# Four edits to a gated-attention and mixer kernel: four first loads, two weight tiles at another place in the queue, four blocks mixed together, and two branch hints

## The chip, the cores and the metric

The kernel runs on 1 core of one Trainium2 chip. The metric is the device time of one execution, in microseconds (us). Three executions of the kernel before took 471.62, 471.79 and 471.83 us; the median is 471.79 us.

## The reference

A linear attention with a forget gate (4 batches, 8 heads, 768 steps, head size 48) is followed by a mixer with a low-rank mix over time and a two-layer channel network (width 384, inner width 1536). In short:

```
f = sigmoid(f_logit)
for t: state = f[t] * state + outer(k[t], v[t]);  y[t] = q[t] @ state
x = y, heads side by side              # (4, 768, 384)
h = (x^T @ U @ V)^T                    # U 768x32, V 32x768: mixes the 768 steps
u = x + h
out = u + relu(u @ w_ch1) @ w_ch2      # w_ch1 384x1536, w_ch2 1536x384
```

q, k, v and f_logit are float32. The weights of the mixer are float64 in HBM.

## The kernel before

The 32 (batch, head) pairs are handled two at a time, as 16 units of two heads, four units for each batch. A unit is loaded as f, k, q and v, the gates are turned into logs and summed over time with a triangular matrix on PE (line 790), keys and queries are turned by PE (line 744) and scaled by DVE (line 758), and then come scores (926), kept keys (953), states (974), the scan over chunks on DVE (996), and the two products that give y (1012 and 1030). ACT moves results out of PSUM and takes the logs and exponentials. The first four units, batch 0, run alone; from then on the attention of batch b+1 is filled in between the matrix products of the mixer of batch b. PE, ACT and DVE follow an order written out by hand for the first batches, and PE for the whole program; later DVE and ACT are ordered by a scheduler, in which the additions of the mixer are given priority (`add`).

**The start.** Line 640 clears `blank`, 384 columns of zeros. PE multiplies it with itself three times (`busy(3)`, line 1133) to have something to do while the first f is loaded. `load(0, "f", "k", "q")` (line 641) issues two DMAs for f, one for each head, then one for k and one for q, all on the queue of SP. Unit 0 treats its f in two halves of three blocks each: DVE clamps them (line 775), ACT takes Exp and Ln (777 and 779), and PE sums them (790).

**The weights.** `weight_loader` (line 82 to 101) brings a float64 tile in and ACT, DVE and POOL turn it into float32. U is `weights[0]`, V is `weights[1:3]`, and the 12 tiles of w1 follow. The first six of these go into room that is not yet in use, tiles of the pool `zp` called `zw`: two of them are asked for at once and issued after V of unit 3's loads (end of the branch `n == 1`), the other four in `held()`, where a copy by ACT of one element of `x` (line 1150) makes SP wait until that point of ACT's program. SP issues its DMAs in order, and waits at most for the one it has to wait for; what stands behind it waits too.

**The mix.** After the low-rank product h (two matmul groups, `low_rank` and `added_up`), `mix(t)` multiplies block t of V with h. There are six blocks of 128 steps; V is stored as four row groups of 32 rows, so blocks 0 to 3 lie in different row groups of PE, and blocks 4 and 5 lie in groups 0 and 1 again. `mix(t)` works in pairs: two blocks go into one PSUM tile of two banks (pool `ps_big`, three such tiles), and DVE adds both to x in one instruction of 768 columns (line 204). For batch 3 the three pairs (`self.mixes`) are laid one by one between the products of the piece before (`fewer`, line 468, a scheme with 15 products in place of 18, whose results DVE combines); the four sums of the next piece (`ready`, 768 columns each) are queued on DVE ahead of all of them.

**The end.** `ok` tells whether the factored path was safe. Each engine reads it into a register (line 1603) and jumps over the general path, which is a second whole program, at line 1604. Then all engines meet and end. POOL, ACT and PE reach their jump long before DVE and SP.

Of the kernel before, what the change touches and what calls it, by code (L numbers as in the profile page):

```python
# [10 lines left out]
F32 = mybir.dt.float32  # L11
# [4 lines left out]
ALU = mybir.AluOpType  # L16
# [140 lines left out]
class Mixer:  # L157
# [6 lines left out]
    def __init__(self, tc, b, x, U, V, w1, w2, sums, ident, blocks, out, two, three, zp, ps_big, ps_mm, wide=False,  # L164
                 z_all=None, room=None, pair=0):
        nc = tc.nc
        P = nc.NUM_PARTITIONS
        NCH, DM = x.shape[1], x.shape[2]
        R, FF = U.shape[2], w1.shape[2]
        NG = P // R  # L170
# [4 lines left out]
        uT, z, h, S = {}, {}, {}, {}  # L175
# [30 lines left out]
        pu = {}  # L206

        def mix(t):

            s = t % 2  # L210
            if s == 0:
                pu[0] = ps_big.tile([P, 2, 512], F32, name="pu", tag="big")
            g = slice((t % NG) * R, (t % NG + 1) * R)
            nc.tensor.matmul(pu[0][:, s, 0:DM], lhsT=V[g, t // NG, :], rhs=h[1][g, :], start=True, stop=True)  # L214
            if s == 1:
                add(x[:, t - 1 : t + 1, :], x[:, t - 1 : t + 1, :], pu[0][:, :, 0:DM], ALU.add)


        hs, last = {}, {}

# [273 lines left out]
            return [(4 * NDC * 2 * P, lambda j=j: ch1(a, j)) for j in range(NI)]  # L494


        parts = [low_rank, added_up, lambda: [mix(t) for t in range(NCH)]]
        parts += [lambda a=a: turn(a) for a in range(NA)]
        self.before = [(DM, piece) for piece in parts]

# [4 lines left out]
        for a in range(NA - 1):  # L505
            ahead = first(a + 1)
            self.main += ready(a) + ahead[: NI // 2] + halved(a) + ahead[NI // 2 :]
        self.main += ready(NA - 1)
        self.after = second(NA - 1)
        self.mixes = [(DM, lambda t=t: [mix(t), mix(t + 1)]) for t in range(0, NCH, 2)]  # L510
        self.first, self.second, self.ready, self.fewer, self.halved = first, second, ready, fewer, halved
        self.sums_of_x = lambda a: [(1, lambda: sums_of_x(a))]

# [24 lines left out]
def factored_path(ctx, tc, q, k, v, f_logit, moe_U, moe_V, moe_w_ch1, moe_w_ch2, out, ok):  # L538
# [4 lines left out]
    nc = tc.nc  # L543
    B, H, S, D = q.shape
    P = nc.NUM_PARTITIONS
    C = P // 2
    NCH = S // C

    NBL = S // P
    HP = H // 2  # L550
    DM = H * D
    R = moe_U.shape[1]
# [21 lines left out]
    ps_big = ctx.enter_context(tc.tile_pool(name="ps_big", bufs=3, space=bass.MemoryType.PSUM))  # L574
    ps_mm = ctx.enter_context(tc.tile_pool(name="ps_mm", bufs=2, space=bass.MemoryType.PSUM))
# [60 lines left out]
                        in_=head[:, :, part * NB : part * NB + n_ch],  # L636
                    )

    blank = late[:, 5, 0 : 3 * P]
    nc.vector.memset(blank, 0.0)  # L640
    load(0, "f", "k", "q")
    load(1, "f")
    load(0, "v")

# [50 lines left out]
    early = len(weights)  # L695
# [10 lines left out]
    FIRST = 6  # L706
# [419 lines left out]
    with tc.manual_schedule(engines={nc.vector.engine, nc.scalar.engine}):  # L1126
# [3 lines left out]

        def busy(n, cols=DM):
            for _ in range(n):
                nc.tensor.matmul(idle[:, 0:cols], lhsT=blank[:, 0:P], rhs=blank[:, 0:cols], start=True, stop=True)

        written = ExitStack()
        written.enter_context(tc.manual_schedule(engines={nc.sync.engine}))
# [7 lines left out]
        halves, join = [[w[i] for w in weights[:early]] for i in (2, 3)]  # L1144
        done, rest = slice(0, 2 * (HP - 1) * D), slice(2 * (HP - 1) * D, DM)

        def held():
            for i in range(2, FIRST, 2):
                t = zp.tile([P, NFC // 2, 2 * P], F32, name="zw").rearrange("p i t -> p (i t)")
                nc.scalar.copy(t[:, 0:1], x_tiles[0][:, 0, 0:1])  # L1150
                spare.extend([t.bitcast(U64)[:, 0:WP], t.bitcast(U64)[:, WP : 2 * WP]])
            for load_w in weights[early + 2 : early + FIRST]:
                load_w[0]()
            load(HP, "f", "k", "q", "v")

        for n in range(HP):
            last = n + 1 == HP
            pieces = rear(n - 1, "scan") + front(n, "unpack_q", "keys") + rear(n, "spread") + rear(n - 1, "read")
            if last:
                pieces += join[:1] + halves[1:2]  # L1160
            elif n:
                pieces += front(n + 1, "gates")
            pieces += front(n, "queries") + rear(n, "kept")
            if n == 0:
                pieces += [lambda: busy(1, P)] + front(1, "gates", "gates_end") + rear(0, "scores", "mask")
                pieces += front(1, "unpack_k") + rear(0, "states")
            elif last:
                pieces += join[1:2] + halves[2:] + rear(n - 1, "inner") + rear(n, "states")
                pieces += join[2:] + rear(n, "scan") + [held] + rear(n, "scores", "mask")
            else:  # L1170
                pieces += front(n + 1, "gates_end", "unpack_k", "unpack_q") + rear(n - 1, "inner") + rear(n, "states")
            if n + 2 == HP:
                pieces += halves[:1]
            if not last:
                pieces += front(n + 1, "read_back")
                pieces += rear(n, "scan", "scores", "mask") if n else []
                pieces += front(n + 1, "keep")
            for piece in pieces:
                piece()
            if n == 0:  # L1180
                load(2, "k", "q")
                load(3, "f")
                load(2, "v")
            elif n == 1:
                weights[0][0]()
                load(3, "k", "q")
                for load_w in weights[1:early]:
                    load_w[0]()
                load(3, "v")
                for load_w in weights[early : early + 2]:  # L1190
                    load_w[0]()
        m = mixer(0)
        low_rank_of, added_up_of, mix_of, turn_of, ch1_of = m.some
        for load_w in weights[early + FIRST : early + FIRST + 4]:
# [75 lines left out]
    def of(i, kind):  # L1270
        if i >= len(pairs):
            return []
        b, a = pairs[i]
        return getattr(mixers[b], kind)(a)
# [5 lines left out]
    for i in range(len(pairs)):  # L1280
        ahead, behind = of(i + 1, "fewer"), of(i, "second")
        nxt = of(i + 2, "sums_of_x")
        if not ahead:
            todo += behind
            break
        todo += of(i, "ready")
        if i == 0:
            todo += [p for two_of in zip(ahead, low[:2] + mixers[1].mixes) for p in two_of] + behind[:1] + low[3:4] + nxt
        else:
            todo += (low[4:] if i == 1 else []) + ahead[:4] + nxt + ahead[4:5]  # L1290
            if i + 2 < len(pairs):
                todo += behind[:1]
        if i + 2 < len(pairs):
            todo += ahead[5:6] + behind[1:2] + ahead[6:7] + behind[2:3] + ahead[7:] + behind[3:]
        else:
            todo += ahead[5:6] + behind[:1] + ahead[6:] + behind[1:2] + of(i + 1, "ready") + behind[2:]
# [284 lines left out]
@with_exitstack  # L1581
def kernel(
    ctx: ExitStack,
    tc: tile.TileContext,
    q: bass.AP,
    k: bass.AP,
    v: bass.AP,
    f_logit: bass.AP,
    moe_U: bass.AP,
    moe_V: bass.AP,  # L1590
    moe_w_ch1: bass.AP,
    moe_w_ch2: bass.AP,
    out: bass.AP,
):


    nc = tc.nc
    args = (q, k, v, f_logit, moe_U, moe_V, moe_w_ch1, moe_w_ch2, out)
    flag = ctx.enter_context(tc.tile_pool(name="flag", bufs=1))
    ok = flag.tile([1, 1], I32, name="ok")  # L1600
    with ExitStack() as inner:
        factored_path(inner, tc, *args, ok)
    good = nc.values_load(ok[0:1, 0:1], min_val=0, max_val=1)
    with tc.If(good == 0):
        with ExitStack() as inner:
            general_path(inner, tc, *args)

# [29 lines left out]
```

## Time and profile before

One profiled execution took 471.81 us. Its span, from the first to the last instruction, is 470.0 us, so 1.8 us lie around it; the times below are in that span.

| | us | share |
|---|---|---|
| span | 470.0 | |
| PE busy | 456.2 | 97% |
| DVE busy | 352.3 | 75% |
| ACT busy | 165.6 | 35% |
| POOL busy | 54.2 | 12% |
| PE idle, 0 to 10 us | 3.3 | |
| PE idle, 10 to 44 us | 2.2 | |
| PE idle, 44 to 160 us | 0.8 | |
| PE idle, 160 to 320 us | 1.1 | |
| PE idle, 320 to 360 us | 1.0 | |
| PE idle, 360 us to the end | 5.4 | |

A line of a timeline has the start and the duration of a group in us, its engine, its line in the kernel, the operation, what it writes and reads, the number of instructions, and in brackets the idle time of its engine just before it with what ended that idle time. Names that end in q (SPq, DVEq) are the sequencers, which issue DMAs, wait and branch. One float32 matmul of the program shows as two instructions.

### The profile page before, as it was taken

The numbers are of one execution on the slowest core, as the hardware profiler recorded it, in microseconds if no ns is written. First come the engines' busy times: TensorE is split into PE (matmuls) and PEld (weight loads), VectorE is DVE, ScalarE is ACT, GpSimd is POOL, SyncE is SP. The second block draws the span as 40 slices with busy tenths as digits, with TensorE's granted clock in tenths as the row PEclk, the third lists the DMA queues.
The fourth block names the chain that finished last, engine by engine and source line by source line (L and its number), as shares of the span: only waits on it lengthen the run. The fifth ranks groups of instructions, "written<-read, shape, count | busy, mean of one in ns | idle before, by whom it ended". The sixth has DMA issues, their size and how long they took to land.

```text
span 470.0 us, 13005 instructions
## 1 busy us (share of the span) xinstructions
PE 456.2 (97%) x5639; PEld 394.9 (84%) x5639; DVE 352.3 (75%) x579; ACT 165.6 (35%) x315; POOL 54.2 (12%) x60
## 2 busy tenths in 40 slices
PE   7999999999999999999999999999999999999995
PEld 5876888875666578999898878989979999999995
DVE  5767788979999677775675659977796877759632
ACT  5775776562332144322323133232312312112200
POOL 2002445634112001010101001020000000000000
PEclk9999999999999999999999999999999999999999
DMA  9947997577678504506334020000000000000001
GB/s 194 209 107 191 226 220 179 155 116 106 120 120 130 83 18 52 77 7 110 48 66 73 7 52 19 12 3 20 18 1 1 35 1 35 0 16 20 1 36 40
DMA packets 148313, 34.36 MB, mean 73 GB/s; under 512 B 136790, under 2 KB 146710, under 8 KB 148246
## 3 DMA queue, kind: packets, MB, share of 16 engines
q1 hardware_dynamic: 148246, 33.44, 36.4%
q8 instruction: 46, 0.75, 0.7%
q14 instruction: 21, 0.17, 0.1%
HBM read 28.70 MB, written 4.72 MB: 71 GB/s over the span
## 4 chain that ended last, share of the span: by engine, by line
PE 75%; DVE 13%; issue 3%; ACT 3%; DMA 2%; SPq 2%; POOL 0%; DVEq 0%; ACTq 0%; POOLq 0%
PE pw L365 25%; PE pz L279 18%; PE pp L468 12%; PE po L331 5%; PE y L1012 2%; PE y L1030 2%; PE ds L974 1%; PE sc L926 1%; PE pt L744 1%; PE pt L790 1%; SPq L634 1%; PE pu L214 1%; DVE late L845 1%; DMA v_nat<-in_v_dram 1%; DVE kz L721 1%
## 5 line engine op out<-in xcount | busy, mean ns | idle before, releaser
L279 PE MATMUL pz<-uT,w 128*128 128x256 f32 x492 | 111.5, 382 | 0.3
L279 PEld LDWEIGHTS pz<-uT,w 128*128 128x128 f32 x492 | 91.7, 190 | 12.9 <-ACT uT L268 0.6
L1000 POOL COPY st<-added 128x576 f32<-128x576 f32 x12 | 18.2, 1513 | 188.0 <-DVE added L996 188.0
L365 PE MATMUL pw<-zw,w_raw 128*128 128x192 f32 x216 | 38.0, 329 | 0.0
L365 PE MATMUL pw<-w,z_all 128*128 128x192 f32 x216 | 37.3, 327 | 0.0
L101 POOL TENSOR_TENSOR w<-w_y,w_r 128x384 int32<-128x384 int32 x24 | 31.5, 1313 | 39.5 <-DVE w_y L100 23.2
L365 PEld LDWEIGHTS pw<-w,z_all 128*128 128x128 f32 x216 | 35.3, 190 | 0.5
L365 PEld LDWEIGHTS pw<-zw,w_raw 128*128 128x128 f32 x216 | 35.1, 190 | 0.6 <-issue 0.3
L314 ACT ACTIVATE z_all<-pz 128x512 f32<-128x512 f32 x33 | 19.6, 598 | 45.1 <-PE pz L279 44.6
L827 DVE TENSOR_TENSOR_SCAN late<-fz,late 128x768 f32<-128x768 f32 x12 | 21.1, 1756 | 7.3 <-ACT fz L822 7.1
L461 ACT ACTIVATE other<-other 128x512 f32<-128x512 f32 x18 | 11.3, 631 | 40.3 <-DVE other L204 40.3
L331 PE MATMUL po<-w,zw 128*128 128x384 f32 x72 | 25.2, 495 | 0.0
L331 PE MATMUL po<-w,z_all 128*128 128x384 f32 x72 | 24.7, 493 | 0.0
L939 DVE TENSOR_TENSOR A<-sc,causal 128x768 f32<-128x768 f32 x16 | 15.2, 952 | 9.5 <-PE sc L926 9.5
L845 DVE TENSOR_TENSOR_SCAN late<-fz,other 128x768 f32<-128x768 f32 x12 | 22.0, 1834 | 0.2
L331 PEld LDWEIGHTS po<-w,zw 128*128 128x128 f32 x72 | 13.2, 190 | 9.6 <-issue 0.8
L331 PEld LDWEIGHTS po<-w,z_all 128*128 128x128 f32 x72 | 13.3, 190 | 8.9 <-DVE o L204 0.6
L981 ACT COPY added<-ds 48x576 f32<-48x576 f32 (+1 forms) x28 | 17.8, 635 | 5.1 <-PE ds L974 4.7
L461 ACT ACTIVATE z_all<-z_all 128x512 f32<-128x512 f32 x12 | 7.6, 630 | 33.3 <-DVE z_all L204 33.3
L468 PE MATMUL pp<-v_nat,late 128*128 128x128 f32 x152 | 19.1, 275 | 0.0
L1012 PEld LDWEIGHTS y<-st,qT 48*64 48x64 f32 x704 | 13.6, 137 | 6.4 <-issue 3.9
L98 DVE TENSOR_SCALAR w_y<-w_y 128x384 f32<-128x384 f32 (+3 forms) x27 | 12.1, 448 | 8.9 <-ACT w_y L91 8.9
(224 smaller groups left out, 867.3 us busy)
## 6 DMA issues: line engine op xcount, KB each, us to landing
w_raw<-in_moe_w_ch_dram SPq DMA_DIRECT2D x18, 384.0 KB, 4.1
out_dram<-o SPq DMA_DIRECT2D x24, 192.0 KB, 2.0
v_nat<-in_v_dram SPq DMA_DIRECT2D x16, 144.0 KB, 4.3
v_nat<-in_v_dram SPq DMA_DIRECT2D x32, 72.0 KB, 3.9
zw<-in_moe_w_ch_dram SPq DMA_DIRECT2D x6, 384.0 KB, 5.1
w<-in_k_dram SPq DMA_DIRECT2D x4, 288.0 KB, 3.7
w<-in_q_dram SPq DMA_DIRECT2D x4, 288.0 KB, 5.1
late<-in_f_logit_dram SPq DMA_DIRECT2D x10, 96.0 KB, 3.0
```

Source lines behind the costliest of these rows:

```text
L101: nc.gpsimd.tensor_tensor(dst.bitcast(I32), shaped(y.bitcast(I32)), shaped(r), ALU.add)
L279: nc.tensor.matmul(pm[:, i * 2 * P : (i + 1) * 2 * P], lhsT=w1[:, m, o : o + P], rhs=uT[a][:, m, :], start=(m == 0), stop=(m == NDC - 1))
L314: nc.scalar.activation(z[a, c][:, k : k + 2, :].rearrange("p i t -> p (i t)"), pm, AF.Relu)
L331: nc.tensor.matmul(pm, lhsT=z[a, i // NI][:, i % NI, s * P : (s + 1) * P], rhs=w2[:, i, :], start=(i == 0), stop=(i == NFC - 1))
L365: nc.tensor.matmul(W["pm"][:, n * HM : (n + 1) * HM], lhsT=lhs[:, i, :], rhs=rhs[:, i, :], start=(i == 0), stop=(i == NI - 1))
L461: nc.scalar.activation(dst, dst, AF.Relu, scale=float(SIGNS[n]))
L468: nc.tensor.matmul(pm[:, i, r * P : (r + 1) * P], lhsT=room["w"](wn)[:, r * P : (r + 1) * P], rhs=x_node(a, xn), start=((xn, wn) == of[0]) ...
L827: nc.vector.tensor_tensor_scan(backwards(X, S - 1, S), backwards(f, S, S), backwards(ends, S - 1, S), 0.0, ALU.mult, ALU.add,)
L845: nc.vector.tensor_tensor_scan(Y, f[:, 0:S], starts, 0.0, ALU.mult, ALU.add)
L981: nc.scalar.copy(added[r, 1:].rearrange("p (e c s) -> p e c s", c=NBL, s=2), ds[r, :, 0 : NBL * D].rearrange("p s (c e) -> p e c s", e=D),)
L1000: nc.gpsimd.tensor_copy(st, states.rearrange(by_e, c=NCH))
L1012: nc.tensor.matmul(o(c % 2, par, c // 2), lhsT=T["q"][rows[par], chunk[c]], rhs=T["st"][rows[par], c, :], start=(c <= 2), stop=False, skip ...
```

## The change

1. **Four first loads.** f of unit 0 comes in four DMAs in place of two: for each half (three blocks) one DMA for each head, the one head on the queue of SP, the other on that of ACT. `blank` is one column, which the busy matmuls read again and again (`broadcast_to`).
2. **V and the first two w1 tiles.** Their loads move from the end of the round n == 1 to the head of the round n == 3. In SP's program V now stands behind v of unit 3, and the two w1 tiles wait for a new one-element copy by ACT, which stands behind the copy of line 808 of unit 3.
3. **Four blocks at once.** For batches 2 and 3, `mix_four` puts blocks 0 and 1 into one tile of `ps_big` and blocks 2 and 3 into one tile each of `ps_mm`; DVE adds 768, 384 and 384 columns. Blocks 4 and 5 go as before. For batch 3 there are two pieces between the products in place of three, and `ready` moves behind one more product piece; in DVE's program the last of its four sums moves from ahead of the products' combinations to behind the additions of blocks 2 and 3.
4. **Hints.** A hint that the jump of line 1604 will be taken, on DVE and SP. It has no dependences: in the built program it is the first instruction of both engines.

```diff
+        def mix_product(dst, t):
+            g = slice((t % NG) * R, (t % NG + 1) * R)
+            nc.tensor.matmul(dst, lhsT=V[g, t // NG, :], rhs=h[1][g, :], start=True, stop=True)
+
+        def mix_four():
+            big = ps_big.tile([P, 2, 512], F32, name="pu", tag="big")
+            pms = [big[:, s, :] for s in range(2)] + [ps_mm.tile([P, 512], F32, name="pu1", tag="mm") for _ in range(2)]
+            for t, pm in enumerate(pms):
+                mix_product(pm[:, 0:DM], t)
+            add(x[:, 0:2, :], x[:, 0:2, :], big[:, :, 0:DM], ALU.add)
+            for t in range(2, NG):
+                add(x[:, t, :], x[:, t, :], pms[t][:, 0:DM], ALU.add)
+
+        def mix_blocks():
+            first = 0
+            if b > 1 and sums is not None:
+                mix_four()
+                first = NG
+            for t in range(first, NCH):
+                mix(t)
...
-        parts = [low_rank, added_up, lambda: [mix(t) for t in range(NCH)]]
+        parts = [low_rank, added_up, mix_blocks]
...
-        self.mixes = [(DM, lambda t=t: [mix(t), mix(t + 1)]) for t in range(0, NCH, 2)]
+        self.mixes = [(DM, mix_four), (DM, lambda: [mix(t) for t in range(NG, NCH)])]
...
-    blank = late[:, 5, 0 : 3 * P]
+    blank = late[:, 5, 0:1]
     nc.vector.memset(blank, 0.0)
-    load(0, "f", "k", "q")
+    queues = nc.sync, nc.scalar
+    for m in range(2):
+        some = slice(m * NBL // 2, (m + 1) * NBL // 2)
+        for par in range(2):
+            queues[par].dma_start(out=nat[0]["f"][:, some, par, 0:D],
+                                  in_=f_logit[0, par].rearrange("(c p) d -> p c d", p=P)[:, some, :])
+    load(0, "k", "q")
...
-                nc.tensor.matmul(idle[:, 0:cols], lhsT=blank[:, 0:P], rhs=blank[:, 0:cols], start=True, stop=True)
+                nc.tensor.matmul(idle[:, 0:cols], lhsT=blank.broadcast_to((P, P)), rhs=blank.broadcast_to((P, cols)),
+                                 start=True, stop=True)
...
-        def held():
-            for i in range(2, FIRST, 2):
+        def room_for(first, last):
+            for i in range(first, last, 2):
                 t = zp.tile([P, NFC // 2, 2 * P], F32, name="zw").rearrange("p i t -> p (i t)")
                 nc.scalar.copy(t[:, 0:1], x_tiles[0][:, 0, 0:1])
                 spare.extend([t.bitcast(U64)[:, 0:WP], t.bitcast(U64)[:, WP : 2 * WP]])
-            for load_w in weights[early + 2 : early + FIRST]:
+            for load_w in weights[early + first : early + last]:
                 load_w[0]()
+
+        def held():
+            room_for(2, FIRST)
             load(HP, "f", "k", "q", "v")
...
             if last:
-                pieces += join[:1] + halves[1:2]
+                pieces = [w[0] for w in weights[1:early]] + [lambda: room_for(0, 2)] + pieces + join[:1] + halves[1:2]
...
                 load(3, "k", "q")
-                for load_w in weights[1:early]:
-                    load_w[0]()
                 load(3, "v")
-                for load_w in weights[early : early + 2]:
-                    load_w[0]()
...
-        todo += of(i, "ready")
         if i == 0:
-            todo += [p for two_of in zip(ahead, low[:2] + mixers[1].mixes) for p in two_of] + behind[:1] + low[3:4] + nxt
+            todo += [p for two_of in zip(ahead, low[:2] + mixers[1].mixes) for p in two_of] + ahead[4:5]
+            todo += of(0, "ready") + behind[:1] + low[3:4] + nxt
         else:
-            todo += (low[4:] if i == 1 else []) + ahead[:4] + nxt + ahead[4:5]
+            todo += of(i, "ready") + (low[4:] if i == 1 else []) + ahead[:4] + nxt + ahead[4:5]
...
+    tc.mark_branch_hint_location("general", "LikelyTaken", engines=[nc.vector.engine, nc.sync.engine])
     good = nc.values_load(ok[0:1, 0:1], min_val=0, max_val=1)
-    with tc.If(good == 0):
+    with tc.If(good == 0, label="general"):
```

## The prediction

> **What bounds the kernel now.** I read the page first, then PE's waits, then the chain of waits, and the timeline wherever a wait of PE lies in the stretch of an edit.
>
> ```profile
> PE 456.2 (97%) x5639; PEld 394.9 (84%) x5639; DVE 352.3 (75%) x579; ACT 165.6 (35%) x315; POOL 54.2 (12%) x60
> PE   7999999999999999999999999999999999999995
> ```
>
> PE is full except in the first and the last slice: 13.8 us of the span are idle, at the front, at the end and in a few gaps. No edit removes PE work, so each can win only a gap. The granted clock is full in every slice. PE's waits name the gaps:
>
> ```profile
> PE pt L790 <- ACT late L779: 1.2, 1, 1.2
> PE sc L926 <- issue: 1.0, 1, 1.0
> ...
> PE pu L214 <- DVE x L204: 0.6, 1, 0.6
> PE pp L468 <- DVE qT L204: 0.4, 1, 0.4
> ```
>
> The columns are the total, the count and the longest. The first is the start, the second a wait that nothing in the profile explains, the last two the mix of batch 3. The chain of waits shows the start (start and duration in us):
>
> ```profile
> 1.32 3.39 DMA late<-in_f_logit_dram
> ...
> 4.81 0.32 DVE late L775
> ...
> 5.16 0.45 ACT late L777
> ...
> 5.63 0.45 ACT late L779
> ...
> 6.17 1.71 PE pt L790 x12
> ```
>
> **What the Trainium skill says.** "Runtime: NRT & Kernel Launch", section "Instruction fetch mechanics": instructions come in blocks of 16 KiB by DMA, the next one during the current one, and a taken branch to a block outside the window has to fetch before it goes on. The trace agrees: the jumps over the general path cost 2.6 us and more (below), each with packets of instructions on queue q14. "DMA: Bandwidth & Descriptors", section "Issuing engines are not separate DMA queues": a second issuing engine saves issue time only. SP's two issues for f take 1.04 us together; the trace has no other queue to compare. "TensorE: Matmul & The Clock Gate", section "Part 3: Packing small matmuls — row/col tiling": matmuls in different row groups run together. The trace agrees: in batch 2's mix eight instructions in four groups took 0.93 us, and four in two groups 0.91. No page prices the branch hint.
>
> **Edit 1, first loads: 0.9 us.** The first f DMA landed at 3.61 and the second, issued behind it, at 4.71; DVE waits for both. With the second head's first half issued by ACT at the same time and half the bytes in each, I put both at the landing of the first, 3.6. The steps to PE are 1.46 us (4.71 to 6.17), so L790 starts at about 5.05. Its second half needs ACT's second Exp and Ln, now back to back behind the first, so the 1.70 us of L790 stay and it ends at 6.75 in place of 7.87: up to 1.1. What is late next is v of unit 0, landed at about 10.6 and used by the states of line 974 at 11.60, and SP's k and q, issued as before. Lower bound: a second DMA on the same 16 engines that lands half a microsecond later, 0.5; upper 1.15, the excess of the wait. ACT issues two DMAs ahead of its table load (1.28 us), which then ends before 4.0, hidden by DMA time. The smaller memset (0.38 us on DVE) is hidden by the same. The 1 us reaches PE only if later unit loads keep up: k, q and f of units 1 to 3 land 0.5 to 0.6 us before their use, but then DVE has waits of 1.3 for ACT, which take it up. I take 0.9.
>
> **Edit 2, w1 tiles: 0.95 us.** From the timeline:
>
> ```profile
> 24.68 1.29 SPq L82 DMA_DIRECT2D zw<-in_moe_w_ch_dram  x2
> 30.21 0.27 PE L926 MATMUL sc<-qT,kz 48*64 48x64 f32 x1 [0.98 <-issue]
> ```
>
> Two tiles of 384 KB go out at 24.68, fill the 16 engines to 95% in 26 to 28 us, and their traffic ends at 30.2. A score matmul waits 0.98 us at just that time for nothing but issue; one packet of 16 KB of instructions lies in 26 to 28. I read a late instruction block. The tiles now wait for a copy by ACT behind L808 (30.03 to 30.23 before, 0.9 earlier with edit 1; the copy takes 0.19), so go out at about 29.5 and 30.15, and land, at the median of 5.1 us of this form, at 34.6 and 35.3. ACT turns them (L91) at 36.37 and 39.34; less 1.85 us of gain ahead, at 34.5 and 37.5. So the first is 0.1 late. That is hidden: what stands behind it on ACT and is wanted soon is the copy of h at L227 (37.31 to 37.71), which PE uses at 39.17, 1.5 us later; the turned w is used at 48.9. At the slowest landing of the six (7.4) it is 2.4 late, which costs 0.9. The copy itself lies in 1.56 us of ACT's idle time. V goes behind v of unit 3, three DMAs, and its first half is turned on ACT at 32.55, well after they land. Bounds: +0.98 for the whole wait; below, 0.98 gained, 0.9 lost to the late tile, 1.0 lost if the next instruction block lies behind the tiles in its turn: −0.9. I take 0.95, since DMA stands empty from 30.4 to 34 in the run before.
>
> **Edit 3, the mix of batch 3: 1.8 us.** The timeline:
>
> ```profile
> 342.02 0.92 PE L214 MATMUL pu<-h,V 32*128 32x384 f32 x4
> ...
> 343.15 0.69 DVE L204 TENSOR_TENSOR qT<-pp,A 128x512 f32<-128x512 f32 x1
> ...
> 343.38 1.13 PE L468 MATMUL pp<-st,fz 128*128 128x128 f32 x8 [0.44 <-DVE qT L204]
> ...
> 344.95 0.95 DVE L204 TENSOR_TENSOR x<-x,pu 128x768 f32<-128x768 f32 x1
> ...
> 345.95 0.91 PE L214 MATMUL pu<-h,V 32*128 32x384 f32 x4 [0.55 <-DVE x L204]
> ...
> 349.62 0.59 PE L365 MATMUL pw<-w,other 128*128 128x192 f32 x2
> ```
>
> Three pair mixes of 0.91 with three products (1.98 each, two lines of x8) between, two waits. I replay it. Four blocks go at 342.02 to 342.95 (the 0.93 of batch 2): one pair's 0.91 is gone. qT (0.69 at 343.15) comes 0.87 earlier, as the fourth sum of 768 columns stands behind it, so ends at 342.97 and the product runs 342.95 to 344.93 without its 0.44. The next mix needs DVE's add of the first 768 columns; it starts at 344.1 in place of 344.95 and is done by 345.0, so the last pair runs 345.0 to 345.85 and its 0.55 is gone. The last product ends at 347.83 and the pw matmuls start there, not at 349.62: 1.8 (0.9 + 0.44 + 0.45). On DVE two adds of 384 columns replace one of 768, 0.1 more; the moved sum has to be done before the products that read it, and DVE has 1.94 us idle behind this stretch. PE is gapless from 349.6 to 464.6, so the gain reaches the end. Bounds: 0.9 for the missing pair alone, 2.0. Batch 2: pairs at 0.93 and 0.91 stay as many, a wait of 0.13 between goes: 0.
>
> **Edit 4, hints: 1.4 us.** The jump line of each sequencer (counts, durations in ns, first and last start):
>
> ```profile
> L1604 POOLq COMPARE_BRANCH  x1: 45/45/45, 322.6 to 322.6; - x1
> L1604 POOLq EVENT_SEMAPHORE  x1: 17/17/17, 325.2 to 325.2; - x1
> ...
> L1604 DVEq COMPARE_BRANCH  x1: 72/72/72, 465.3 to 465.3; - x1
> L1604 SPq COMPARE_BRANCH  x1: 50/50/50, 465.4 to 465.4; - x1
> ...
> L1604 DVEq EVENT_SEMAPHORE  x1: 21/21/21, 468.5 to 468.5; - x1
> ```
>
> POOL's next instruction comes 2.6 us after its jump and DVE's 3.2; SP's is at 468.1, 2.7 after (ACT, at 455.4, 2.7 too). The last store is issued at 465.03 and its data has landed by 467.0 (median of that form 2.0). Without the jumps' fetch SP would wait for the store to 467.0, then SP's semaphores (0.5 before, 468.1 to 468.6) and the closing 1.35 us (468.65 to 470.0): 468.6 in place of 470.0, 1.4. Upper bound 1.7, where the semaphores pass at once; lower bound 0, and below nothing by one fetch, since the hint is the first instruction of both engines, 460 us ahead of the jump.
>
> **Sum:** 471.81 − 0.9 − 0.95 − 1.8 − 1.4 = 466.76, so 466.8. The profiled run is within 0.02 us of the median.
>
> **The rivals.** *B, the hint does nothing* (target dropped by the blocks that follow): 466.8 + 1.4 = 468.2. For it: the distance, some 340 instructions on SP and 740 on DVE. Against: each engine has this one jump to keep in mind. No trace here has a hinted jump. *C, the early gains don't carry* (edits 1 and 2 are taken back by the DMA or DVE chain between 88 and 135 us, where the chain of waits goes through v's DMAs at 118.9 and 131.1): 466.8 + 1.85 = 468.6. Against: PE waits only 0.81 us in 44 to 160. *D, both*: 470.0. *E, slower*: the hint takes the place of the sequential fetch, so that DVE and SP stop for a block. DVE has some 740 instructions, three blocks, and each stop costs what a jump does, 2.65 us. Exposed on PE they outweigh the 3.65 us of the other edits from the second one on; with three it is 471.8 − 3.65 + 7.95 = 476.1. For it: the wait of edit 2 shows that a late block can stop an engine. Against: DVE has 1.9 us of idle time and more at many places, and of PE's other waits on issue the longest is 0.6 us (line 974).
>
> **Chances.** All four as worked out (466.1 to 467.3) 0.52; B (467.5 to 468.9) 0.24; C 0.10; D 0.06; E 0.05; below 466.0 0.03. The range 465.9 to 468.9 takes in the case of all, B and C's middle, and the sums of the lower bounds of edits 1 and 3 (466.8 + 0.4 + 0.9 = 468.1). A measurement tells 0.2%, 0.94 us, from no change: everything except D's upper part and E is faster by more.
>
> **What would show it.** Edit 1: L790 starts at about 5.1 and its wait of 1.2 shrinks to about 0.1; if the DMA of ACT's queue lands at 4.5, the step fails. Edit 2: no PE wait of 0.98 on "issue" at 29 to 30, and no wait of L91 for zw of over 0.2 us; a new issue wait at 31 to 35 would show the fetch behind the tiles. Edit 3: the two L204 waits gone, pw 5.6 us behind the start of the four-block mix rather than 7.6. Edit 4: DVE and SP's next instruction within 0.2 us of the jump and the span's end 3.5 us after the last store is issued, not 5.0. Rival C shows as new PE waits in 88 to 135, E as DVE sitting 2 us on "issue" in mid-program. The forecast is wrong if the hint needs to stand near its branch, or if a first half waits for the other head.

## The result and the profile after

The changed kernel took 467.49 us (median of 6 executions, 467.18 to 469.12); the kernel before, run beside it, 471.81 us. The ratio is 0.991 with an interval of 0.989 to 0.993. The forecast of 466.8 us is 0.7 low, and the time lies in the range. The profiled execution took 467.36 us with a span of 465.5, so again 1.8 us lie around it. One execution of sums_first, 475.68 us at a mean granted clock of 0.984, was in a slower state than all others and is left out below.

The page's first lines and PE's waits of the changed kernel (behind line 214 its lines are numbered 21 to 28 higher than before; 790 is now 817, 926 is 953, 365 is 386, 468 is 489, 1604 is 1632):

```profile
PE 455.7 (98%) x5639; PEld 395.0 (85%) x5639; DVE 352.7 (76%) x581; ACT 165.8 (36%) x316; POOL 54.4 (12%) x60
PE   8999999999999999999999999999999999999996
```

```profile
PE y L1039 <- DVE st L1023: 0.8, 1, 0.8
...
PE sc L953 <- issue: 0.4, 1, 0.4
...
PE pu L214 <- DVE x L204: 0.2, 1, 0.2
```

The work of PE is the same and its idle time has gone from 13.8 to 9.8 us. The wait of the first sums at the start and the one for qT are gone, the wait on issue is 0.4 where it was 1.0, and that for x 0.15 where it was 0.55.

I set the matmul records of both traces (one for each matmul instruction, numbered from 0) side by side, in the order of PE's program, and read off how far the changed kernel is ahead. That is the sum of the whole change:

```
place (time before, us)                       ahead, us   step   forecast
end of the first sums, line 790 (7.9)            0.62     0.62     0.9
behind the wait on issue, line 926 (30.2)        1.12     0.50     0.95
up to the mix of batch 2 (270.7)                 1.02    -0.10     -
behind the mix of batch 2 (272.7)                1.50     0.48     0
behind the mix of batch 3 (349.9)                3.42     1.92     1.8
end of the span                                  4.45     1.03     1.4
```

The timeline of the start, after (start, duration, engine, line, operation, tiles, form, count, and in brackets the idle time before it):

```profile
3.68 1.01 DVE L802 TENSOR_SCALAR late<-late 128x288 f32<-128x288 f32 x2 [0.35 <-DMA late<-in_f_logit_dram]
...
4.30 0.44 ACT L804 ACTIVATE late<-late 128x288 f32<-128x288 f32 x1 [1.18 <-DVE late L802]
4.78 0.44 ACT L806 ACTIVATE late<-late 128x288 f32<-128x288 f32 x1
...
5.32 1.94 PE L817 MATMUL pt<-later,late 128*128 128x130 f32 x12
```

The first half of f is there at 3.6, as forecast, but ACT begins at 4.30, 0.6 behind the start of the clamp (before, 0.35), and the sums take 1.94 us in place of 1.70.

PE's timeline in the mix of batch 3, after:

```profile
340.51 0.93 PE L221 MATMUL pu<-h,V 32*128 32x384 f32 x8
341.37 1.16 PE L489 MATMUL pp<-st,fz 128*128 128x128 f32 x8
342.36 1.06 PE L489 MATMUL pp<-uT,late 128*128 128x128 f32 x8
343.57 0.91 PE L214 MATMUL pu<-h,V 32*128 32x384 f32 x4 [0.15 <-DVE x L204]
344.42 1.16 PE L489 MATMUL pp<-st,z_all 128*128 128x128 f32 x8
345.41 1.06 PE L489 MATMUL pp<-st,late 128*128 128x128 f32 x8
346.30 0.98 PE L386 MATMUL pw<-w,other 128*128 128x192 f32 x5
```

From the first matmul of the mix to line 386 it is 5.79 us; the same stretch took 7.60 before (342.02 to 349.62). The jump of the changed kernel, with both hints (count, durations in ns, first and last start):

```profile
L1632 SPq EVENT_SEMAPHORE  x8: 17/17/17, 463.6 to 464.2; - x8
...
L1632 DVEq COMPARE_BRANCH  x1: 84/84/84, 461.9 to 461.9; - x1
L1632 SPq COMPARE_BRANCH  x1: 70/70/70, 462.0 to 462.0; - x1
...
L1632 DVEq EVENT_SEMAPHORE  x1: 21/21/21, 462.5 to 462.5; - x1
```

DVE goes on 0.6 us behind its jump, where it was 3.2. SP's waits pass from 463.6 to 464.2; the last store had been issued at 461.6. The span ends 3.9 us behind that issue; before it was 5.0.

### The profile page after: what moved, and what is told of

Same layout as the page of the kernel before. It is cut to its first block, busy times and chain, and to the rows that moved or that the text cites. A ratio compares the mean times of both kernels' runs of the same rounds, so it can differ in the third digit from the quotient of the medians.

```text
span 465.5 us, 13015 instructions
## 1 busy us (share of the span) xinstructions
PE 455.7 (98%) x5639; PEld 395.0 (85%) x5639; DVE 352.7 (76%) x581; ACT 165.8 (36%) x316; POOL 54.4 (12%) x60
## 4 chain that ended last, share of the span: by engine, by line
PE 79%; DVE 12%; ACT 3%; issue 3%; DMA 2%; POOL 0%; SPq 0%; DVEq 0%; ACTq 0%; POOLq 0%
PE pw L386 25%; PE pz L300 21%; PE pp L489 12%; PE po L352 5%; PE y L1039 2%; PE y L1057 2%; PE sc L953 2%; PE pt L771 2%; PE ds L1001 1%; PE pt L817 1%; DVE late L854 1%; PE pt L980 1%; DVE late L907 1%; PE put L288 1%; PE idle L1160 1%
```

## The experiments

Theory: the change is worth what the table shows, each edit by its own mechanism: an earlier f, a block of PE's instructions that no longer lies behind two weight tiles, a mix with fewer stops, and two jumps that don't fetch. Rivals: that one hint is enough or the hints do nothing, that the waits on issue don't come from the tiles, that the later loads take the early start back, and that four blocks at once do in the mix what I gave to DVE's order. All kernels are the changed one with one edit more. Single times spread over 2 us and more, so the medians tell little below 0.5 us, and most verdicts rest on the traces.

**The hints.** Without any, with that of DVE alone, with that of SP alone.

```diff
-    tc.mark_branch_hint_location("general", "LikelyTaken", engines=[nc.vector.engine, nc.sync.engine])
+    # no_hint: the line is left out; hint_dve: engines=[nc.vector.engine]; hint_sp: engines=[nc.sync.engine]
```

> The changed kernel without the hints. Theory (the hints save what the two jumps cost behind the last store): the next instruction of DVE comes 3.2 us behind its jump again and that of SP 2.7 us, the stretch from PE's last matmul to the end grows from 4.3 to 5.4 us, and the time from 467.5 to 468.6 us. Rival (the end is short for another reason, such as a quicker last store): end stretch within 0.3 us of 4.3, time 467.5 us.

> The hint on DVE alone. Theory (each engine pays its own jump and the end waits for the later one): DVE goes on 0.6 us behind its jump, SP 2.7 us; SP then finds all stores landed and is through 0.5 to 0.7 us later than with both hints; end stretch 4.8 to 5.0 us, time 468.1 us. Rival (one hint is enough, since both engines jump to the same place): 467.5 us. Second rival (one hint alone brings nothing, as the other engine still holds the end): 468.6 us.

> The hint on SP alone. Theory: SP goes on at once and waits for the stores, DVE comes 3.2 us behind its jump, 0.9 us later than SP is through; end stretch 5.1 to 5.3 us, time 468.4 us. Rival (one is enough): 467.5 us.

```
             median us (range)            ratio to before [interval]   PE's end to span's end, us
both         467.49 (467.18 to 469.12)    0.991 [0.989, 0.993]         4.36
no_hint      468.81 (468.42 to 470.37)    0.994 [0.992, 0.995]         5.41
hint_dve     468.90 (468.26 to 471.47)    0.995 [0.993, 0.997]         5.49
hint_sp      468.81 (467.48 to 471.26)    0.995 [0.993, 0.996]         4.79
before                                                                 5.38
```

The jump of hint_dve, then that of hint_sp:

```profile
L1632 SPq EVENT_SEMAPHORE  x8: 17/17/17, 464.5 to 465.1; - x8
...
L1632 SPq COMPARE_BRANCH  x1: 50/50/50, 461.8 to 461.8; - x1
L1632 DVEq EVENT_SEMAPHORE  x1: 21/21/21, 462.2 to 462.2; - x1
```

```profile
L1632 SPq EVENT_SEMAPHORE  x8: 17/17/17, 463.5 to 464.1; - x8
L1632 DVEq COMPARE_BRANCH  x1: 72/72/72, 461.6 to 461.6; - x1
...
L1632 DVEq EVENT_SEMAPHORE  x1: 21/21/21, 464.7 to 464.7; - x1
```

Each hint acts on its own engine alone. The fetches agree: from the jumps to the end of the span queue q14 carries four packets of instructions, of 8 KB each, in the kernel before and in no_hint, three in hint_dve and in hint_sp, and two with both hints, so each hint takes one fetch away. Without SP's, SP goes on 2.8 us behind its jump and its eight waits still take 0.55 us (464.5 to 465.1), though the last packet of data of the stores ends at 462.9 in that trace: they are eight steps, not one wait. So DVE's hint alone brings nothing, as the second rival said and my theory of 4.8 to 5.0 us did not. With SP's alone the end waits for DVE at 464.7, 0.7 behind SP: 4.79, less than the 5.1 to 5.3 expected. Both together give 1.05 (5.41 less 4.36). The medians of the three kernels, 468.81 to 468.90, don't tell them apart; the order is read from the traces.

**The weight tiles.**

```diff
             if last:
-                pieces = [w[0] for w in weights[1:early]] + [lambda: room_for(0, 2)] + pieces + join[:1] + halves[1:2]
+                pieces += join[:1] + halves[1:2]
...
                 load(3, "k", "q")
+                for load_w in weights[1:early]:
+                    load_w[0]()
                 load(3, "v")
+                for load_w in weights[early : early + 2]:
+                    load_w[0]()
```

> The changed kernel with V and the first two w1 tiles issued at the old place. Theory (PE's instruction block comes late because the tiles fill the DMA engines): the wait on issue at a score matmul is 0.9 to 1.0 us again in place of 0.42, and the time is 468.0 us. Rival (PE takes blocks faster there than they are fetched, with the tiles or without; the change of the wait was chance): the wait stays at 0.4 us and the time at 467.5 us.

Measured: 468.25 us (467.65 to 469.25), ratio 0.992 [0.991, 0.994], which isn't clear of the changed kernel's. PE's waits of w1_early between 15 and 41 us:

```profile
PE sc L953 <- issue: 1.0, 1, 1.0
PE y L1039 <- DVE st L1023: 0.8, 1, 0.8
PE y L1057 <- issue: 0.4, 1, 0.4
```

The 1.0 is back, as the theory had it, and a second wait has come. This edit moves V's loads and the two tiles together, so it doesn't part their shares. To test the cause further, no_v takes V's traffic away.

```diff
-            dma.dma_start(out=shaped(raw), in_=w)
+            if empty:                                   # empty=True for V
+                nc.gpsimd.memset(raw.bitcast(U32), 0)
+            else:
+                dma.dma_start(out=shaped(raw), in_=w)
```

> The changed kernel leaves out the two loads of V (its raw tiles are set to zero by POOL instead), so less moves between 23 and 27 us. In the profiles so far PE waits on issue at 28.7 to 30.9 us (record 598), or 128 records earlier or later, always 1.2 to 1.6 us behind the end of a 16 KB packet of instructions, and that packet starts 1.3 to 2.9 us after PE has passed the block before. Theory (other DMA traffic makes the packet late): with V's traffic gone the packet behind the block of 24.9 us starts within 1.4 us, PE has no wait on issue above 0.1 us at record 598, and the times are 0.3 to 0.5 us lower and closer together: median 467.0 us. Rival (the fetch itself is as slow as PE's use of a block, traffic or not): the wait at 598 stays 0.2 to 0.4 us and the times as spread as before, 467.2 to 469.1 us.

Measured: 467.49 us (467.04 to 468.57), ratio 0.990 [0.988, 0.992]: no faster, and little closer together. The wait at record 598 is gone, but others stand ahead of it:

```profile
PE sc L956 <- issue: 1.0, 1, 1.0
...
PE y L1060 <- issue: 0.5, 1, 0.5
```

So V's loads are not what is left of it. What is, shows when all profiles are laid together, those of the other experiments too. The records at which PE waits on issue between 15 and 41 us are always the same, 127 apart or twice that (598 stands for 598 or 599, the two instructions of one matmul), and only the share of each changes (one more, of 0.57 us at record 1652, is the same in all fourteen and stays out):

```
wait on issue, us, at matmul record       345    472    598    852    y (line 1012) starts
tiles early:  before                       -      -     0.98    -      38.00
              w1_early                     -     0.42   0.99    -      37.64
              start_old (below)            -     1.43   1.21    -      40.69
tiles late:   after                        -      -     0.42    -      36.83
              after_again (below)          -     0.53    -      -      36.83
              no_hint                     0.75   1.07   0.44   0.13    38.67
              hint_dve                     -      -      -     0.41    36.29
              hint_sp                      -     0.28   0.17    -      36.66
              b2_pairs                     -      -     0.17    -      36.53
              sums_first                   -     0.11    -     0.14    37.04
              pairs_late                   -     0.75    -     0.14    37.62
              f_together                   -     0.56    -      -      37.14
              pool_quiet                  0.30   0.53    -     0.14    37.31
              no_v                        1.02   0.53    -      -      37.76
```

127 matmul records with their 127 weight loads and a few waits are a block of 256 instructions. In the trace's packets each of the 20 waits at 345, 472 and 598 ends 1.2 to 1.6 us behind the end of one packet of 16 KB on PE's instruction queue (before: packet 27.54 to 28.98, PE goes on at 30.21), and where PE passes one of these records without a wait, the packet has ended 1.18 us before or earlier. At record 598 the mean is 1.06 us over the three profiles with the tiles early and 0.11 over the eleven with them late. The packets say the same: from PE's entry into the block at record 472 to the end of the next packet it is 3.2 to 3.5 us with the tiles early and 2.2 to 2.7 with them late. At the other places together the mean wait is 0.6 with the tiles early and 0.7 with them late: there the tiles change nothing. So edit 2 takes off what it was to take off, 0.95 on average at that record, and the block before or behind is late for reasons that the edit doesn't touch and that no experiment here finds.

**The start.** f together, and the memsets of POOL moved.

```diff
-    queues = nc.sync, nc.scalar
-    for m in range(2):
...
-    load(0, "k", "q")
+    load(0, "f", "k", "q")
```

> The changed kernel with f of unit 0 in two DMAs on SP's queue as before (the one-column blank stays). Theory (the chain of the start carries the landing of f through to the end, but for what PE's instruction blocks take back): the first clamp starts at 4.75 us, behind the second DMA, takes 0.32 since POOL has ended by then, PE's first sums start at 6.1 us in place of 5.32, and the score matmul behind them is 0.6 us later than with the split. Rival (the later loads set the pace, so the start is free): PE stands level with the changed kernel again before 20 us, at the same time for the sums of unit 1 or 2. Time 468.1 us by the theory, 467.5 by the rival, both within the spread that the waits on issue make.

Measured: 467.95 us (467.26 to 469.38), ratio 0.993 [0.990, 0.995]. The clamp starts at 4.50 and takes 0.31, the first sums start at 5.85, 0.54 later than with the split, and PE is 0.31 behind at the y products. f itself landed 0.3 us earlier than in the profile of before. PE has not caught up at record 345 (20.69 and 20.40 us), so the rival falls. Of the 0.54, 0.24 went already in the sums, which take 1.70 here and 1.94 in the changed kernel's profile (below).

```diff
     for i in range(2):
-        nc.gpsimd.memset(kz[i][:, 0:C], 0.0)
+        nc.vector.memset(kz[i][:, 0:C], 0.0)
...
-    nc.gpsimd.memset(added[:, 0:1], 0.0)
+    nc.vector.memset(added[:, 0:1], 0.0)
     for i in range(2):
-        nc.gpsimd.memset(wholes[i][:, 0:1], 0.0)
+        nc.vector.memset(wholes[i][:, 0:1], 0.0)
```

> Five small memsets of POOL (kz, added, whole; to 4.1 us) moved to DVE, ahead of the clamp of f. Theory (in all profiles of the split f the first clamp ends at 4.26 to 4.28 us, whenever it began, 0.17 behind POOL's last memset: DVE is held while POOL works): the clamp takes 0.31 to 0.4 us and ends at 4.0 to 4.1, and PE's first sums start at 5.1 in place of 5.32; time 0.2 us lower if no wait on issue takes it. Rival (the clamp's end is set by when f has landed): the clamp still ends at 4.27, at 5.32 PE starts, or all is later by the memsets that DVE has more, 0.3 us.

The timeline of the changed kernel and, behind it, that of pool_quiet, up to 4.3 us:

```profile
3.68 0.58 DVE L802 TENSOR_SCALAR late<-late 128x288 f32<-128x288 f32 x1 [0.35 <-DMA late<-in_f_logit_dram]
...
3.77 0.23 POOL L708 MEMSET kz<- 128x64 f32 x2
...
3.94 0.10 POOL L713 MEMSET added<- 128x1 f32 x1
...
3.97 0.13 POOL L715 MEMSET whole<- 128x1 f32 x2
```

```profile
3.29 0.19 DVE L708 MEMSET kz<- 128x64 f32 x2
...
3.53 0.29 POOL masks.py:199 TENSOR_SCALAR_AFFINE_SELECT ident<-ident 128x128 f32<-128x128 f32 x1
...
3.79 0.31 DVE L802 TENSOR_SCALAR late<-late 128x288 f32<-128x288 f32 x1 [0.28 <-DMA late<-in_f_logit_dram]
...
4.13 0.44 ACT L804 ACTIVATE late<-late 128x288 f32<-128x288 f32 x1 [1.01 <-DVE late L802]
```

The clamp takes 0.31 where POOL has ended and 0.58 beside POOL's memsets; it starts later in pool_quiet and still ends earlier. That fits what the Trainium skill says in "SBUF — State Buffer", section "SBUF: two separate sides": one pair of ports is shared by DVE, for an instruction in its two-port mode, and GpSimd as an exclusive lock; whichever starts first holds it for a whole instruction, and the other blocks. The trace doesn't show in which mode the clamp ran. It can also go the other way: in no_v the clamp starts at 3.66 and takes 0.33, and it is POOL's two memsets of kz that take 0.31 and 0.29 in place of 0.15, while in b2_pairs the clamp starts at 3.56 and takes 0.72. What decides it is open. PE's first sums start at 5.14 in place of 5.32. The time is 467.56 us (466.62 to 468.62), ratio 0.991 [0.988, 0.994]: no gain that can be told, and in the profile the waits at 345 and 472, 0.83 together where the changed kernel has 0.42, cost more than the 0.18.

The other part, the sums' 1.94 us, I read from the spacing of their records: 0.35 and 0.21 us up to 6.1 us, 0.11 behind; in no_hint and hint_sp it is 0.11 from 5.5 on and the sums start at the same time. "TensorE: Matmul & The Clock Gate", section "Part 1: The HAM clock gate", tells that PE begins at half its clock and that the moment of the change differs from run to run. The trace agrees with both: the spacing halves, and the full clock in the trace's record of the granted clock begins at 6.06 us in the changed kernel, 4.89 in hint_sp, 4.25 before, and up to 7.25 in sums_first, where the sums take 2.5 us. By 5.32 us, where the first sums now start, the clock was full in five of the fourteen profiles, by 6.17, where they started before, in ten. So the 0.24 differs from execution to execution, and an earlier start meets the slow clock more often. No experiment sets that moment.

**The mix.** Batch 2 in pairs again (condition `b > 2`); the fourth sum back ahead; and the pairs with the sum behind.

```diff
-            if b > 1 and sums is not None:              # b2_pairs
+            if b > 2 and sums is not None:
```

> Four blocks at once for batch 3 alone, batch 2 in three pairs again. Theory (the third pair waits for the third tile of ps_big until DVE has added the last product that lies in it, and drains of PE's pipeline come on top): from the first to behind the last matmul of batch 2's mix 1.97 us in place of 1.49, all later PE work 0.48 us later, nothing else moved. Rival (the 0.48 us came from four row groups being worked together): the first two pairs take less than 0.95 us also here, and the loss is under 0.15 us. Time 468.0 us by the theory.

Measured: 468.20 us (467.43 to 468.54), ratio 0.993 [0.990, 0.995]. PE's timeline of batch 2's mix in b2_pairs, then in the changed kernel:

```profile
269.35 1.99 PE L214 MATMUL pu<-h,V 32*128 32x384 f32 x12
271.32 0.59 PE L386 MATMUL pw<-w,w_raw 128*128 128x192 f32 x2
```

```profile
269.68 0.93 PE L221 MATMUL pu<-h,V 32*128 32x384 f32 x8
270.43 0.81 PE L214 MATMUL pu<-h,V 32*128 32x384 f32 x4
271.17 0.43 PE L386 MATMUL pw<-w,w_raw 128*128 128x192 f32 x1
```

1.97 us to line 386 in pairs, 1.49 with four at once. In b2_pairs the first two pairs also take 0.93 and the third comes 1.07 behind the first, with a wait of 0.14 in front of it, and takes 0.90; without a wait the next group starts 0.75 behind the first and is done after 0.74. DVE's addition of the last product that lay in PSUM ends 0.15 us ahead of the third pair's start (271.62 and 271.77 before). A stop thus costs its 0.14 and twice some 0.17 here, which I read as a pipeline that has run empty; that reading isn't tested. The rival of the row groups falls: the first two pairs are as quick as the four blocks, and the loss is there.

```diff
         if i == 0:
-            todo += [p for two_of in zip(ahead, low[:2] + mixers[1].mixes) for p in two_of] + ahead[4:5]
-            todo += of(0, "ready") + behind[:1] + low[3:4] + nxt
+            todo += of(0, "ready") + [p for two_of in zip(ahead, low[:2] + mixers[1].mixes) for p in two_of] + ahead[4:5]
+            todo += behind[:1] + low[3:4] + nxt
```

> Four blocks at once in both batches, but the fourth sum of batch 3 back ahead of the products on DVE. Theory (half of edit 3 in batch 3 is the pair of matmuls that goes, half is DVE's order): PE waits again for qT and for the addition to x, together 0.8 to 0.9 us, and the mix of batch 3 with its three products takes 6.6 to 6.7 us in place of 5.8; time 468.4 us. Rival (four blocks alone do it, the order of the sums is cover): no wait of PE above 0.2 us there, time 467.5 us.

```diff
-        self.mixes = [(DM, mix_four), (DM, lambda: [mix(t) for t in range(NG, NCH)])]
+        self.mixes = [(DM, lambda t=t: [mix(t), mix(t + 1)]) for t in range(0, NCH, 2)]
...
-            todo += [p for two_of in zip(ahead, low[:2] + mixers[1].mixes) for p in two_of] + ahead[4:5]
+            todo += [p for two_of in zip(ahead, low[:2] + mixers[1].mixes) for p in two_of]
```

> Batch 3 in three pairs as before the change, but the fourth sum stays behind on DVE (batch 2 keeps four at once). From the first matmul of the mix to the product of line 386 behind it: 7.6 us before, 7.4 with four blocks and the sums first, 5.8 in the changed kernel. Theory (the place of the sum removes the waits for qT and x, 0.9 to 1.0 us, and four at once the pair, 0.8 to 0.9, which shows only once the waits are gone): 6.6 to 6.7 us, time 468.4 us. Rival (the place of the sum does it all, four blocks at once are worth nothing): 5.8 to 6.0 us, time 467.5 us. Second rival (only both together help, since the pairs wait for their PSUM tiles whatever DVE's order): 7.4 us or more, time 469.2 us.

```
mix of batch 3 to line 386, us         sum ahead   sum behind
three pairs                              7.60        6.74
four blocks, then two                    7.42        5.79
```

sums_first took 469.61 us (468.65 to 470.18), ratio 0.995 [0.993, 0.997]; pairs_late 469.17 us (468.45 to 469.27), ratio 0.993 [0.990, 0.995]. PE's timeline of sums_first, then of pairs_late:

```profile
340.99 0.93 PE L221 MATMUL pu<-h,V 32*128 32x384 f32 x8
342.36 1.13 PE L489 MATMUL pp<-st,fz 128*128 128x128 f32 x8 [0.44 <-DVE qT L204]
...
345.22 0.91 PE L214 MATMUL pu<-h,V 32*128 32x384 f32 x4 [0.84 <-DVE z_all L204]
346.55 1.13 PE L489 MATMUL pp<-st,z_all 128*128 128x128 f32 x8 [0.41 <-DVE x L204]
...
348.41 0.65 PE L386 MATMUL pw<-w,other 128*128 128x192 f32 x3
```

```profile
341.55 0.91 PE L214 MATMUL pu<-h,V 32*128 32x384 f32 x4
...
344.61 0.91 PE L214 MATMUL pu<-h,V 32*128 32x384 f32 x4 [0.17 <-DVE x L204]
...
348.28 0.59 PE L386 MATMUL pw<-w,other 128*128 128x192 f32 x2
```

Four blocks alone are worth 0.18 us, the place of the sum alone 0.86, and both 1.81. With the sum ahead PE is held for 1.69 us by DVE, twice what I expected, and the stretch takes 7.42 in place of the 6.6 to 6.7 of the theory: the pair that is saved only lets PE come to DVE's results sooner. Part of the 1.69 may have another cause: in sums_first DVE's scheduler also put the additions of the two single blocks (343.92 and 344.98) ahead of that of the first 768 columns, which ends at 346.40; in the changed kernel the latter comes first. So the 0.18 is for four blocks with that order, and the share of the order isn't parted. For pairs_late the theory's 6.6 to 6.7 is nearly met; its time, 469.17 for 468.4, is not, with first sums of 2.46 us and 0.89 of waits on issue in its profile.

**Edits 1 and 2 together, and the kernel once more.** start_old undoes f_together's and w1_early's parts and has `blank` with 384 columns; after_again is the changed kernel.

> The changed kernel with edits 1 and 2 undone together (f in two DMAs, blank of 384 columns, V and the first two w1 tiles at their old place); the mixes and hints stay. Theory (edits 1 and 2 bring 0.6 and 0.5 us, what the profiles of before and after show at the record where the waits on issue end): PE reaches the y products behind the scan of unit 3 at 37.8 to 38.2 us in place of 36.8, with a wait on issue of 0.9 to 1.0 at record 598 or 599, and the time is 468.6 to 468.8 us. Rival (the waits on issue take back the earlier start, so that the two edits together bring nothing on average): y products at 36.9 to 37.3, time within 0.4 us of the changed kernel beside it.

> The changed kernel once more, for a second profile and times beside the others. Theory (its spread comes from the waits on issue between 15 and 40 us): median 467.5, range 467.2 to 469.1 us; the waits on issue in the profile sum up to another value than 0.42 us, and the span differs from 465.5 us by just that difference and up to 0.3 us of the first sums' slower start. Rival (spread from elsewhere, such as the landing of the last store or the mixes): the waits are the same and the span is not.

On one chip start_old took 468.72 us (467.45 to 470.77; ratio 0.994 [0.992, 0.996]) and after_again 467.71 (466.46 to 470.16; 0.993 [0.990, 0.996]): 1.0 us between the medians, as the theory had it, with intervals that overlap. start_old's y products come at 40.69 us, not at 37.8 to 38.2. In after_again the wait on issue is 0.53 at record 472 and none at 598; record 599 comes at 29.09 in both profiles, and both spans are 465.5. So neither form of the last expectation held: the wait had moved, and the span stayed. The first sums of after_again end at 7.01, 0.86 ahead of the kernel before and not 0.62, and at record 345, the first of the block borders, the lead over the first profile is gone again. start_old's profile is from its slowest execution. Two waits on issue, 1.43 and 1.21, lie close together there, and behind them PE's granted clock drops (window and its length, the busy times of PE, PEld, DVE, ACT and POOL with their counts, the clock, the DMA share and GB/s):

```profile
32.00:34.00 2.00, 2.00 (x51) 1.71 (x51) 1.79 (x3) 0.39 (x1) 0.00 (x0) 1.00 0.03 9
34.00:36.00 2.00, 2.00 (x18) 1.60 (x16) 1.09 (x5) 0.58 (x3) 0.59 (x1) 0.50 0.00 0
36.00:38.00 2.00, 2.00 (x90) 1.88 (x90) 1.76 (x6) 1.41 (x4) 0.45 (x1) 0.65 0.03 8
```

PE falls 1.3 us further behind in that stretch. That explains this profile. For the other high times there is only the mean granted clock of each execution. The highest times of hint_dve, hint_sp, f_together, pool_quiet and after_again come with the lowest clock of their kernels (0.994 to 0.996), which fits such a stretch; those of the changed kernel (469.12), w1_early, b2_pairs and no_v come with 1.0, so they have another cause.

## Why the prediction was right, point by point

- **Bound and gaps.** Right: PE was full, no edit changed its work, and each won a gap. The likeliest case came, all four edits act; but 467.49 us lies above the 466.1 to 467.3 given for it and at the edge of rival B's 467.5, so the time alone couldn't tell the two apart. The traces and no_hint do.
- **Edit 1, 0.9 forecast, 0.62 measured.** The landing was right (3.6). The term that failed is "the steps to PE are 1.46 us", with the sums' 1.70 behind it. The clamp took 0.58 in place of 0.32, since at 3.7 POOL is still at its memsets where at 4.8 it wasn't (shown by pool_quiet), and the sums 0.24 longer at PE's early clock (read from the spacing and the clock record, not tried). 1.12 less 0.26 and 0.24 is the 0.62. It was carried whole to 28 us in this profile. In after_again, where the clock was full earlier, 0.86 was won and 0.23 of it lost at record 345.
- **Edit 2, 0.95 forecast, 0.50 in the pair of profiles.** The mechanism was right, a late block behind the tiles. The term that was too simple is that the wait stands at one record: it is one of four, whose share changes from run to run. At the record itself the gain is 0.95 on average, over three profiles with the tiles early and eleven with them late. No new wait came at 31 to 35. The tiles went out at 29.73, near the 29.5 forecast, and had landed by 33.3 and 34.9; ACT turns them from 35.19 and 38.25, with no wait for a DMA among its waits.
- **Batch 2, 0 forecast, 0.48 measured.** Failed: "pairs at 0.93 and 0.91 stay as many, a wait of 0.13 between goes". I took a group's duration as its cost. The cost is the distance to the next group, 0.75 here without a stop.
- **Batch 3, 1.8 forecast, 1.81 measured** to the first matmul of line 386. The replay held as a whole. Its split did not: "0.9 for the missing pair alone" as a lower bound is wrong, for alone it is 0.18 (with the order of additions of sums_first). The replay was right since it walked PE and DVE together. (Its text counts three products between the pairs; there are two, as its own times use.)
- **Edit 4, 1.4 forecast, 1.03 measured.** The mechanism was right, and both hints are needed. The sum was wrong: 467.0 + 0.5 + 1.35 is 468.85, not 468.6, so the step's own terms give 1.15. Of its signs, "within 0.2 us of the jump" came as 0.6 for DVE (SP's next instruction is a wait, so its own can't be read), and 3.5 us behind the last store's issue as 3.9.
- **Rivals.** B falls with no_hint. C doesn't hold in the pair (0.1 lost up to 270 us). E falls: the longest wait of DVE on issue is 0.2 us, as before. The gains that fell short (0.28 + 0.45 + 0.37) and the 0.1 lost up to 270 us come to 1.2 us; the gains that weren't forecast (0.48 + 0.12) make up half of that. So the total, 4.45 for 5.05, is nearer than its parts, and that is luck.

## What to carry to other kernels

Where two engines hand work to and fro, walk both together through the stretch with the new order: the part that looks like the gain (one group of matmuls less) was worth 0.18 us alone and 0.95 once the other engine's order let it count. Take as a group's cost on PE the distance to the next group: here a stop of 0.14 us cost 0.48. A wait on "issue" that stands at fixed distances in PE's program, in every kernel of a family, was here a block of instructions coming late; moving big loads away cleared one block, and a single profile of such a kernel can be 1 to 2 us off another.

## What the runs showed of the hardware that was not expected

- A hint that stands first in an engine's program, 460 us and some 740 instructions of DVE ahead of its jump, still took the jump from 3.2 to 0.6 us, on that engine alone, and one packet of instructions of 8 KB less was fetched behind the jump.
- PE's instruction blocks came late by up to 1.43 us where it runs small matmuls beside loaded DMA queues, and PE went on 1.2 to 1.6 us behind the end of the block's packet. "Runtime: NRT & Kernel Launch", section "Instruction fetch mechanics", calls the cost of crossing a block mostly hidden; between 15 and 40 us of this kernel it isn't.
- In one profile two such waits (1.43 and 1.21) within 5 us were followed by a stretch at a granted clock of 0.50, which cost 1.3 us.
- A clamp of DVE beside a row of POOL's memsets took 0.45 to 0.72 us in place of 0.31, in nine of the ten profiles in which they met; in the tenth it took 0.33 and the memsets were held.
- Eight semaphore waits of SP that are all met take 0.55 us.
